# Residual weights of the second matrix by accumulating transfers, and other planned times for the first units

## The chip, the cores and the metric

The kernel runs on one core of one Trainium2 chip. The metric is the device time of one execution, in microseconds (us). The kernel before takes 532.01 us (median of three runs, 531.34 to 532.36).

The engines are called as in the profile: PE multiplies matrices, DVE, ACT and POOL work element by element, and SP starts the transfers from and to memory. Each engine runs its own instructions in the order in which they were issued, and waits on semaphores for the others.

## The reference

Sliding-window attention (each row sees itself and the 63 rows before it) feeds a gated two-matrix layer with a convolution of width 3 along the sequence:

```
scores = scale * q @ k.T ; masked to 0 <= rel < 64 ; softmax ; x = attn @ v      # B=8, H=8, S=576, D=64
h      = max(x @ w_in, 0)                                                        # 512 -> 1024
conv   = sum_k conv_w[k] * shifted(h, k - 1)
out    = (h * sigmoid(conv)) @ w_out                                             # 1024 -> 512
```

The weights `w_in`, `conv_w` and `w_out` come as 64-bit words and are turned into 32-bit floats on the chip.

## The kernel before, in words

**Units.** The 4608 rows are cut into 12 units of 384 rows. For each unit: scores (`qk`), row maxima (`row_max`), exponentials (`exps`), normalising, a transposition, attention times values (`values`), the first matrix (`mm1`), the rectifier (`relu`), the convolution (`conv_mid` on ACT, `conv_side` on DVE), the sigmoid and gate (`sig`, `gate`), and the second matrix (`mm2`). The score work of unit u+2 runs beside the matrices of unit u. Units 0 and 1 come out of a start-up stretch in which the weights are prepared too. Their transposition is on PE (`transpose_pe`), that of later units on DVE with small transfers. Scores of units 0 and 1 use 64-row pieces, those of later units 32-row pieces (64 matmuls a block, three blocks a unit).

**Large and small parts.** A 32-bit operand is multiplied as a large part, rounded to PE's fast format, and a small part, the difference to it. Each product is three matmuls: large times large, small weight times large, large weight times small. So `wih`, `woh` hold large parts of the weights and `wil`, `wol` the small parts; `xh`, `xl` and `gh`, `gl` do the same for activations.

**Weights.** A chunk of weights is two of the eight 128-row slices (the first two slices of `w_in` are chunks of their own). `to_f32` makes floats of the 64-bit words in a buffer `w24`, of which there are two: an absolute value and a scaling on ACT (L248, L255), a maximum on POOL (L249), and a shift, an or and an add on DVE (L250, L252, L256). Then POOL rounds the result to the large part (L269, `CAST`) and DVE subtracts it from the whole (L270), which gives the small part. `w_out` is four chunks; chunk n+2 uses the `w24` buffer of chunk n again.

**The order.** Every piece of work is put into a plan with a due time, an engine, a cost, what it reads and what it writes. `START` holds due times, in units of one eighth of a unit's work, for the start-up and for units 0, 1 and later ones. `queued` simulates the engines with the costs and always starts, on the engine that is free first, the ready work with the lowest due time; the order so found is issued as it stands. [...] While PE would wait in the first 110 us, `keep_busy` (L212) puts matmuls on zeros into the gap; their results are not used.

Of the kernel before, what the change touches and what calls it, by code (L numbers as in the profile page):

```python
# [8 lines left out]
F32 = mybir.dt.float32  # L9
F32R = mybir.dt.float32r  # L10
U32 = mybir.dt.uint32
AF = mybir.ActivationFunctionType
ALU = mybir.AluOpType
# [47 lines left out]
def queued(works, fill=None):  # L61
# [30 lines left out]
    while left:  # L92
# [17 lines left out]
        if fill and e == "PE" and start < FILL_TO:  # L110
# [4 lines left out]
            if n > 0 and clean:  # L115
                order.append(Work(x.t, e, 0.0, fill(n, min(clean)[1]), [], [], None, 0, 0.0))
        turn = SWITCH[e] if e in SWITCH and (x.kind != state[e] if e == "PE" else x.kind and x.kind != state[e]) else 0.0
        if turn and e == "PE" and not x.kind:
            turn = LEAVE
        if e == "PE" or x.kind:  # L120
# [17 lines left out]


START = {  # L140
    "v0": -27.5,
    "pv0": -15.968,
    "conv": -37.437,
    "bits": ((-46.561, -47.419), (-44.383, -45.007)),
    "qk1": -43.011,
    "v1": -11.849,
    "qk2": -2.185,
    "qk0": (-91.154, -52.794, -48.024),
    "ex0": (-42.377, -37.771, -19.993),
    "sc1": (-20.012, -18.408, -14.041),  # L150
    "ex1": (-8.106, -4.046, -3.778),
    "mask": -0.529,
    "sig": ((3.087, 7.079, 8.764, 10.751), (3.178, 6.73, 5.945, 9.966), (4.046, 6.806, 8.285, 10.314)),
    "in": (-39.031, -37.38, -33.878, -12.682, -12.013),
    "out": (-11.963, -8.679, 1.926, 7.315),
# [3 lines left out]
}  # L159
SWITCH = {"PE": 0.14, "ACT": 1.28}  # L160
LEAVE = 0.24
PORT_CL = 0.5
WARM = 5.0
FILL, FILL_FROM, FILL_TO = 4.0, 2.0, 110.0

# [2 lines left out]
def attention_moe(ctx: ExitStack, tc: tile.TileContext, q, k, v, w_in, conv_w, w_out, out):  # L168
    nc = tc.nc
# [4 lines left out]
    def many(n, shape, dt, name, where=pool):  # L174
        return [where.tile(shape, dt, name=f"{name}{i}") for i in range(n)]
# [7 lines left out]
    mask = many(3, [P, P], F32, "mask")  # L183
# [13 lines left out]
    bits = [flat.bitcast(U32)[:, 4 * DM * i:4 * DM * (i + 1)].rearrange("p (e two) -> p e two", two=2) for i in range(2)]  # L197
# [20 lines left out]
    def at(t, eng, cost, do, r=(), w=(), kind=None, mb=0, port=0.0):  # L218

        plan.append(Work(t, eng, cost, do, list(r), list(w), kind, mb, port))  # L220

    def two(t, eng, cost, do, **kw):
        at(t, eng, cost, do, port=cost, **kw)
# [20 lines left out]
    def to_f32(t, n, st, x, kb, kt):  # L244

        lw, hw, xu = st[..., 0], st[..., 1], x.bitcast(U32)

        at(t, "ACT", 0.0009 * n + 0.2, lambda: nc.scalar.activation(x, hw.bitcast(F32), AF.Abs), r=kb, w=kt)  # L248
        at(t, "POOL", 0.0027 * n + 0.02, lambda: nc.gpsimd.tensor_scalar(x, x, TINY, None, op0=ALU.max), w=kt, port=PORT_CL)  # L249
        two(t, "DVE", 0.00052 * n + 0.06, lambda: nc.vector.tensor_scalar(  # L250
            xu, xu, 3, 0x3FFFFFF8, op0=ALU.logical_shift_left, op1=ALU.bitwise_and), w=kt)
        two(t, "DVE", 0.00104 * n + 0.07, lambda: nc.vector.scalar_tensor_tensor(  # L252
            xu, hw, 0xC0000000, xu, op0=ALU.bitwise_and, op1=ALU.bitwise_or), r=kb, w=kt)

        at(t, "ACT", 0.0009 * n + 0.2, lambda: nc.scalar.activation(lw, lw, AF.Copy, scale=2.0 ** -29), w=kb)  # L255
        two(t, "DVE", 0.00104 * n + 0.07, lambda: nc.vector.tensor_tensor(xu, xu, lw, ALU.add), r=kb, w=kt)  # L256

    def weights(t, src, fs, hi, lo, key, buf, halves):

        e = slice(halves[0] * DM, (halves[-1] + 1) * DM)  # L260
        st, x = bits[buf][:, e], w24[buf][:, e]
        kb, kt = [("bits", buf, a) for a in halves], [("w24", buf, a) for a in halves]
        for f, a, tl in zip(fs, halves, load_at(buf, halves, t)):
            at(tl, "SP", 0.7, lambda f=f, a=a: nc.sync.dma_start(
                bits[buf][:, a * DM:(a + 1) * DM], src[f].bitcast(U32).rearrange("p (e two) -> p e two", two=2)),
               w=[("bits", buf, a)], mb=0.52)
        n = len(fs) * DM
        to_f32(t, n, st, x, kb, kt)
        two(t, "POOL", 0.00127 * n, lambda: nc.gpsimd.tensor_copy(hi, x), r=kt, w=[f"{key}{f}h" for f in fs])  # L269
        two(t, "DVE", 0.00104 * n + 0.07, lambda: nc.vector.tensor_tensor(lo, x, hi.bitcast(F32), ALU.subtract),  # L270
           r=kt + [f"{key}{f}h" for f in fs], w=[f"{key}{f}l" for f in fs])

    freed = {}

    def load_at(buf, halves, t):

        ts = [freed.get((buf, a), START["bits"][buf][a]) for a in halves]
        for a in halves:
            freed[(buf, a)] = t + 0.01
        return ts  # L280

    def weights_in(t, fs, *where):
        f = slice(fs[0], fs[-1] + 1)
        weights(t, w_in, fs, wih[:, f].rearrange("p f c e -> p (f c e)"),
                wil[:, f].rearrange("p f c e -> p (f c e)"), "in", *where)

    def weights_out(t, fs, *where):
        f = slice(fs[0], fs[-1] + 1)
        weights(t, w_out, fs, woh[:, f].rearrange("p f e -> p (f e)"), wol[:, f].rearrange("p f e -> p (f e)"), "out", *where)
# [441 lines left out]
```

## Time and profile before

| what | before |
|---|---|
| median of 3 runs | 532.01 us (531.34 to 532.36) |
| the profiled execution: own time, span | 531.34 us, 529.6 us |
| PE busy, share of the span | 518.5 us, 98% |
| DVE busy | 380.3 us, 72% |
| ACT busy | 379.7 us, 72% |
| POOL busy | 112.6 us, 21% |
| matmuls on zeros (L212) | 210, 28.6 us of PE's busy time |
| granted TensorE clock | 1.00 |

The profiled execution is the fastest of the three runs, 0.67 us under their median, and 1.7 us of its own time lie outside its span. A busy PE here is not always useful: the matmuls on zeros count as busy, so the gaps of the start-up are to be sought as L212 rows and not as idle time alone. Line numbers in the profile are those of the kernel before. In the changed kernel the lines behind L269 are moved by five: L270 there is the `CAST` of L269, L273 to L276 are new, and L506, say, is L501 here.

### The profile page before, as it was taken

The page shows a single profiled execution, that of the slowest core. Times are in us where ns is not written, and L with a number is a line of the kernel's source. Part 1 is how long each engine was busy: PE and PEld are TensorE (multiplying, and loading weights), DVE is VectorE, ACT ScalarE, POOL GpSimd, SP SyncE. Part 2 cuts the span into 40 slices and gives each one's busy share as a digit, 9 for nine tenths or more (in the row PEclk, how much of TensorE's full clock was granted, in tenths as well). Part 3 has the DMA queues.
Part 4 walks back from the last instruction along what each step waited for, and adds up shares of the span by engine and source line. Part 5 has one row for each costly group of instructions (what it writes and reads, how often), then busy time and mean ns, then how long its engine had stood idle before and what let it go on. Part 6 is the DMA issues. An engine that isn't in the chain of part 4 may idle for free.

```text
span 529.6 us, 14836 instructions
## 1 busy us (share of the span) xinstructions
PE 518.5 (98%) x5826; PEld 499.8 (94%) x5826; DVE 380.3 (72%) x1084; ACT 379.7 (72%) x1011; POOL 112.6 (21%) x196
## 2 busy tenths in 40 slices
PE   9998999999999999999999999999999999999996
PEld 8887889999999999999999999999999999999996
DVE  3899999985858667767767767767767667655552
ACT  2997897579896696696697687687687687544542
POOL 6664467113131011021021021021021021000000
PEclk9999999999999999999999999999999999999999
DMA  8984660237292173183083074073073053010011
GB/s 284 365 296 136 208 231 1 60 109 248 76 325 72 58 256 83 42 291 77 21 297 77 16 253 122 21 285 105 13 264 120 17 152 104 16 61 0 2 60 62
DMA packets 29463, 69.98 MB, mean 132 GB/s; under 512 B 5713, under 2 KB 17617, under 8 KB 29393
## 3 DMA queue, kind: packets, MB, share of 16 engines
q1 hardware_dynamic: 29392, 69.03, 39.7%
q8 instruction: 46, 0.75, 0.6%
q14 instruction: 25, 0.20, 0.1%
HBM read 47.73 MB, written 9.47 MB: 108 GB/s over the span
## 4 chain that ended last, share of the span: by engine, by line
PE 85%; DVE 9%; DMA 1%; ACT 1%; issue 1%; SPq 1%; POOL 0%; DVEq 0%
PE po L564 39%; PE acc L501 36%; PE acc L481 6%; PE sc L350 5%; DVE c L535 1%; DVE w L252 1%; DMA T<-in_w_in_dram 1%; DVE s L357 1%; DVE w L256 1%; DVE wil L270 1%; ACT s L367 1%; SPq L234 1%; DVE xl L488 1%; DVE s L378 1%; DVE w L250 1%
## 5 line engine op out<-in xcount | busy, mean ns | idle before, releaser
L501 PE MATMUL acc<-xh,wih 128*128 128x384 f32 x384 | 131.5, 342 | 0.8 <-DVE xl L488 0.8
L564 PE MATMUL po<-gh,woh 128*128 128x386 f32 (+1 forms) x384 | 132.1, 344 | 0.0
L535 DVE SCALAR_TENSOR_TENSOR c<-hbuf,cw,c 128x386 f32<-128x386 f32 (+1 forms) x192 | 109.6, 623 | 30.7 <-ACT c L528 30.7
L564 PE MATMUL po<-gh,wol 128*128 128x386 f32 (+1 forms) x384 | 129.9, 338 | 0.0
L564 PE MATMUL po<-gl,woh 128*128 128x386 f32 (+1 forms) x384 | 129.7, 338 | 0.0
L501 PE MATMUL acc<-xh,wil 128*128 128x384 f32 x384 | 129.7, 338 | 0.0
L501 PE MATMUL acc<-xl,wih 128*128 128x384 f32 x384 | 129.7, 338 | 0.0
L367 ACT ACTIVATE s<-s,nm 128x96 f32<-128x96 f32 (+2 forms) x288 | 105.1, 367 | 5.2 <-DVE nm L357 4.9
L555 DVE TENSOR_TENSOR gl<-c,gh 128x772 fp32r<-128x772 f32 (+1 forms) x48 | 55.8, 1162 | 28.2 <-ACT gh L551 28.1
L501 PEld LDWEIGHTS acc<-xh,wih 128*128 128x128 f32 x384 | 72.1, 188 | 2.9 <-POOL sm L370 0.7
L564 PEld LDWEIGHTS po<-gh,woh 128*128 128x128 f32 x384 | 72.2, 188 | 2.6
L378 POOL TENSOR_TENSOR s<-s,r 128x768 f32<-128x768 f32 x27 | 39.7, 1472 | 163.5 <-DVE r L373 150.7
L547 DVE TENSOR_TENSOR c<-c,hbuf 128x772 f32<-128x772 f32 (+1 forms) x48 | 47.4, 987 | 36.9 <-ACT c L542 36.7
L564 PEld LDWEIGHTS po<-gl,woh 128*128 128x128 f32 x384 | 72.3, 188 | 0.0
L564 PEld LDWEIGHTS po<-gh,wol 128*128 128x128 f32 x384 | 72.3, 188 | 0.0
L501 PEld LDWEIGHTS acc<-xh,wil 128*128 128x128 f32 x384 | 72.2, 188 | 0.0
L501 PEld LDWEIGHTS acc<-xl,wih 128*128 128x128 f32 x384 | 72.1, 188 | 0.0
L522 ACT ACTIVATE hbuf<-acc 128x384 f32<-128x384 f32 x64 | 30.9, 486 | 45.8 <-PE acc L501 45.4
L542 ACT ACTIVATE c<-c 128x772 f32<-128x772 f32 (+1 forms) x48 | 40.7, 848 | 30.2 <-DVE c L535 29.9
L357 DVE CUSTOM_DVE_ANT_0 s<-sc,mask 128x96 f32<-128x96 f32 (+2 forms) x272 | 51.5, 254 | 9.7 <-POOL mask L321 5.7
L367 ACT ACTIVATION_READ_ACCUMULATOR s<-s,nm 128x1 f32 x288 | 54.3, 189 | 0.0
L511 POOL COPY hbuf<-hbuf 128x4 f32<-128x4 f32 x44 | 16.7, 379 | 176.3 <-DVE c L547 176.2
(64 smaller groups left out, 644.5 us busy)
## 6 DMA issues: line engine op xcount, KB each, us to landing
v<-in_v_dram SPq DMA_DIRECT2D x24, 768.0 KB, 7.2
ub<-T SPq DMA_DIRECT2D x240, 48.0 KB, 1.9
k<-in_k_dram SPq DMA_DIRECT2D x22, 448.0 KB, 4.9
q<-in_q_dram SPq DMA_DIRECT2D x22, 384.0 KB, 6.9
out_dram<-T SPq DMA_DIRECT2D x8, 772.0 KB, 4.2
T<-in_w_in_dram SPq DMA_DIRECT2D x8, 512.0 KB, 6.6
T<-in_w_out_dram SPq DMA_DIRECT2D x8, 512.0 KB, 4.2
out_dram<-T SPq DMA_DIRECT2D x3, 768.0 KB, 6.4
```

The lines of the kernel that those rows point to most:

```text
L350: nc.tensor.matmul(banks_of(u, b)[h][r:r + rows, i * P + o:i * P + n], qs[hs, 2 * g + p, t:t + rows], ks[hs, 2 * g + p, t + o:t + n], star ...
L357: nc.vector.tensor_tensor_reduce(out=ss[b][:, i, h, o:n], in0=banks_of(u, b)[h][:, i * P + o:i * P + n], in1=mask[m][:, o:n], scale=-0.125 ...
L367: nc.scalar.activation(x, x, AF.Exp, bias=nms[b][:, e], scale=-1.0, accum_out=sms[b][:, e])
L378: on.tensor_tensor(sv, sv, rs[b].unsqueeze(2).broadcast_to([P, 2 * NB, n]), ALU.mult)
L481: nc.tensor.matmul(acc[bank(("v", u, c))][h * D:(h + 1) * D, t * W:(t + 1) * W], vs[:, c, t, h], ub[g][:, 2 * p:2 * p + 2, 2 * t + h], sta ...
L501: nc.tensor.matmul(acc[bank(("m", u, f))][:, :NX], w[:, f, c], x[u % 2][:, c], start=(c == 0 and j == 0), stop=(c == NC - 1 and j == 2))
L522: nc.scalar.activation(hbuf[:, f, o:o + NX], ps[:, :NX], AF.Relu)
L535: nc.vector.scalar_tensor_tensor(c, hbuf[:, f, e:e + n], cw[:, e, f:f + 1], c, op0=ALU.mult, op1=ALU.add)
L542: nc.scalar.activation(c, c, AF.Sigmoid)
L547: nc.vector.tensor_tensor(c, c, hbuf[:, 2 * i:2 * i + 2, 1:1 + n], ALU.mult)
L555: nc.vector.tensor_tensor(gls[ring(u, i)][:, :, :n], cs[i % 2][:, :, :n], ghs[ring(u, i)][:, :, :n].bitcast(F32), ALU.subtract)
L564: nc.tensor.matmul(po[o][:, :n], w[:, f, es], x, start=(f == 0 and j == 0), stop=(f == NF - 1 and j == 2))
```

## The change

The small part of `w_out` is no longer subtracted on DVE. ACT writes the negative of the large part to `wol` (L273), and then a transfer that POOL issues (L274) adds the whole from `w24` to it. `w_in` keeps its subtraction on DVE. Beside it stand other due times for the start-up and units 0 and 1 (those of later units are the same), and other costs for the planner: 0.12 and 0.19 for a change of matmul kind in place of 0.14 and 0.24, 0.87 us for the port in L249 in place of 0.5, and 1.06 us for a `CAST` of 1024 in place of 1.30.

```diff
 START = {
-    "v0": -27.5,
+    "v0": -29.922,
 ...
-    "out": (-11.963, -8.679, 1.926, 7.315),
+    "out": (-20.758, -19.305, -17.841, -7.024),
 ...
-SWITCH = {"PE": 0.14, "ACT": 1.28}
-LEAVE = 0.24
-PORT_CL = 0.5
+SWITCH = {"PE": 0.12, "ACT": 1.28}
+LEAVE = 0.19
+PORT_CL = 0.87
 ...
         n = len(fs) * DM
         to_f32(t, n, st, x, kb, kt)
-        two(t, "POOL", 0.00127 * n, lambda: nc.gpsimd.tensor_copy(hi, x), r=kt, w=[f"{key}{f}h" for f in fs])
-        two(t, "DVE", 0.00104 * n + 0.07, lambda: nc.vector.tensor_tensor(lo, x, hi.bitcast(F32), ALU.subtract),
-           r=kt + [f"{key}{f}h" for f in fs], w=[f"{key}{f}l" for f in fs])
+        his, los = [f"{key}{f}h" for f in fs], [f"{key}{f}l" for f in fs]
+        two(t, "POOL", 0.00104 * n, lambda: nc.gpsimd.tensor_copy(hi, x), r=kt, w=his)
+        if key == "out":
+            at(t, "ACT", 0.0009 * n + 0.12, lambda: nc.scalar.activation(lo, hi.bitcast(F32), AF.Copy, scale=-1.0), r=his, w=los)
+            at(t + 0.005, "POOL", 1.2, lambda: nc.gpsimd.dma_start(lo, x, accum_op=ALU.add), r=kt, w=los, mb=0.9)
+        else:
+            two(t, "DVE", 0.00104 * n + 0.07, lambda: nc.vector.tensor_tensor(lo, x, hi.bitcast(F32), ALU.subtract), r=kt + his, w=los)
```

Three places where the order differs. First POOL, around the large part of the first chunk of `w_out` (`woh`; `w240` and `w241` are the two `w24` buffers), before:

```order
L249 TENSOR_SCALAR w240_101<-w240_101 128x1024
L249 TENSOR_SCALAR w241_102<-w241_102 128x1024
L511 COPY hbuf_67<-hbuf_67 128x2x2
L513 MEMSET hbuf_67 128x2
L411 MEMSET ub1_62 32x2x384
L412 MEMSET ub1_62 32x2x384
L269 CAST woh_70<-w240_101 128x1024
```

and in the changed kernel:

```order
L270 CAST wih_68<-w241_102 128x1024
L270 CAST woh_70<-w240_101 128x1024
L249 TENSOR_SCALAR w241_102<-w241_102 128x1024
L274 DMA wol_71<-w240_101 128x1024
L516 COPY hbuf_67<-hbuf_67 128x2x2
L518 MEMSET hbuf_67 128x2
L270 CAST woh_70<-w241_102 128x1024
L274 DMA wol_71<-w241_102 128x1024
L249 TENSOR_SCALAR w240_101<-w240_101 128x1024
```

The transfer stands behind the maximum of the next chunk, and the rounding of the first chunk now follows that of the last chunk of `w_in` at once.

Second DVE, from the last row maximum of unit 2's second block to the last small part of unit 1's `x`, before (`wol` is the subtraction; a row of L488 makes a quarter of `xl`):

```order
L250 TENSOR_SCALAR w241_102<-w241_102 128x1024
L555 TENSOR_TENSOR gl0_97<-c0_92,gh0_94 128x772
L252 SCALAR_TENSOR_TENSOR w241_102<-T_100,w241_102 128x1024
L488 TENSOR_TENSOR xl1_66<-acc0_106,xh1_64 128x384
L488 TENSOR_TENSOR xl1_66<-acc1_107,xh1_64 128x384
L535 SCALAR_TENSOR_TENSOR c0_92<-hbuf_67,cw_72,c0_92 128x386 x2
L270 TENSOR_TENSOR wol_71<-w240_101,woh_70 128x1024
L256 ISA w241_102<-T_100,w241_102 128x2048
L535 SCALAR_TENSOR_TENSOR c0_92<-hbuf_67,cw_72,c0_92 128x386 x2
L488 TENSOR_TENSOR xl1_66<-acc0_106,xh1_64 128x384
L547 TENSOR_TENSOR c1_93<-c1_93,hbuf_67 128x772
L270 TENSOR_TENSOR wol_71<-w241_102,woh_70 128x1024
```

and in the changed kernel:

```order
L250 TENSOR_SCALAR w241_102<-w241_102 128x1024
L560 TENSOR_TENSOR gl0_97<-c0_92,gh0_94 128x772
L252 SCALAR_TENSOR_TENSOR w241_102<-T_100,w241_102 128x1024
L493 TENSOR_TENSOR xl1_66<-acc0_106,xh1_64 128x384
L540 SCALAR_TENSOR_TENSOR c1_93<-hbuf_67,cw_72,c1_93 128x386 x2
L256 ISA w241_102<-T_100,w241_102 128x2048
L540 SCALAR_TENSOR_TENSOR c1_93<-hbuf_67,cw_72,c1_93 128x386 x2
L493 TENSOR_TENSOR xl1_66<-acc0_106,xh1_64 128x384
L540 SCALAR_TENSOR_TENSOR c0_92<-hbuf_67,cw_72,c0_92 128x386 x2
L552 TENSOR_TENSOR c1_93<-c1_93,hbuf_67 128x772
L540 SCALAR_TENSOR_TENSOR c0_92<-hbuf_67,cw_72,c0_92 128x386 x2
L493 TENSOR_TENSOR xl1_66<-acc0_106,xh1_64 128x384
```

The two subtractions are gone from between the other rows.

Third ACT in the changed kernel, from the first negation (L273) to the second (L527 is the rectifier of `mm1`, L490 makes a quarter of `xh`, L248 is here the first step of the third chunk in the buffer `w240`):

```order
L490 CAST xh1_64<-acc0_106 128x384
L273 ACTIVATE wol_71<-woh_70 128x1024
L527 ACTIVATE hbuf_67<-acc1_107 128x384
L556 CAST gh0_94<-c0_92 128x772
L527 ACTIVATE hbuf_67<-acc1_107 128x384
L533 ACTIVATE c0_92<-hbuf_67,cw_72 128x386 x2
L255 ACTIVATE T_100<-T_100 128x1024
L527 ACTIVATE hbuf_67<-acc1_107 128x384
L490 CAST xh1_64<-acc0_106 128x384
L248 ACTIVATE w240_101<-T_100 128x1024
L547 ACTIVATE c1_93<-c1_93 128x772
L273 ACTIVATE wol_71<-woh_70 128x1024
```

A rectifier stands directly behind the first negation, and the third chunk's first write to `w240`, which the first transfer reads, stands ahead of the second.

More of the change, by code (lines that the diff above doesn't have):

```diff
@@ L140 @@
 START = {
-    "v0": -27.5,
[L142 to L154, printed above, removed]
-    "out": (-11.963, -8.679, 1.926, 7.315),
[3 rows of a table removed]
-}
-SWITCH = {"PE": 0.14, "ACT": 1.28}
-LEAVE = 0.24
-PORT_CL = 0.5
+    "v0": -29.922,
+    "pv0": -19.403,
+    "conv": -41.041,
+    "bits": ((-47.782, -46.477), (-39.599, -42.604)),
+    "qk1": -50.73,
+    "v1": -11.363,
+    "qk2": -8.864,
+    "qk0": (-89.193, -55.235, -53.427),
+    "ex0": (-43.48, -40.099, -25.648),
+    "sc1": (-9.472, -21.051, -12.204),
+    "ex1": (-7.956, -5.445, -5.217),
+    "mask": -7.074,
+    "sig": ((2.956, 5.48, 6.549, 10.868), (2.942, 5.419, 7.756, 9.491), (4.046, 6.806, 8.285, 10.314)),
+    "in": (-47.207, -43.911, -35.394, -25.628, -25.348),
+    "out": (-20.758, -19.305, -17.841, -7.024),
[3 rows of a table added]
+}
+SWITCH = {"PE": 0.12, "ACT": 1.28}
+LEAVE = 0.19
+PORT_CL = 0.87
 WARM = 5.0
```

6 rows, old and new, of the table START are left out of this document.

## The prediction

> **What bounds the kernel now.** First the busy shares, then busy time by stretch, since shares are averages over stages; then PE's instructions in order of time where the stretches change, and last the chain of waits.
>
> ```profile
> PE 518.5 (98%) x5826; PEld 499.8 (94%) x5826; DVE 380.3 (72%) x1084; ACT 379.7 (72%) x1011; POOL 112.6 (21%) x196
> ...
> 0.00:69.73 69.73, 28.56 (x210) 26.39 (x210) 1.00 0.75 260
> ...
> 69.73:96.57 26.84, 26.60 (x168) 1.00 0.23 78
> 96.57:530.00 433.43, 428.93 (x4713) 1.00 0.36 115
> ...
> 512.82 12.69 PE po L564 x72
> ```
>
> The first stretch row is of L212 alone (window, its length, PE, weight loads), the two below are of all of PE. All 210 zero matmuls, 28.56 us, lie ahead of 69.73 us. From there PE loses 0.24 us to 96.57, and from 96.57 to its last matmul (512.82 + 12.69 = 525.51) it is busy 428.93 of 428.94 us. The end is therefore the time at which PE becomes steadily fed, plus the PE work still to do. Only the start-up can move it, as the due times of later units are unchanged.
>
> ```profile
> 50.00:60.00 10.00, 9.69 (x135) 9.07 (x134) 10.00 (x26) 7.65 (x13) 7.29 (x3) 1.00 0.49 153
> 60.00:70.00 10.00, 8.50 (x164) 7.65 (x164) 10.00 (x27) 9.20 (x22) 3.05 (x5) 1.00 0.91 306
> 70.00:80.00 10.00, 9.76 (x74) 9.37 (x70) 10.00 (x14) 9.06 (x35) 6.97 (x5) 1.00 0.56 190
> 80.00:90.00 10.00, 10.00 (x58) 10.00 (x58) 9.52 (x13) 8.79 (x18) 8.07 (x7) 1.00 0.00 0
> ...
> 66.14 2.93 PE L212 MATMUL po<-spare 128*128 128x112 f32 x24
> 69.73 0.92 PE L481 MATMUL acc<-ub,v 128*64 128x64 f32 x24 [0.66 <-DVE xl L488]
> 70.58 0.44 PE L501 MATMUL acc<-xh,wih 128*128 128x384 f32 x1
> 70.86 0.34 PE L501 MATMUL acc<-xh,wil 128*128 128x384 f32 x1
> 71.04 0.34 PE L501 MATMUL acc<-xl,wih 128*128 128x384 f32 x1
> ...
> 71.20 1.14 DVE wol L270
> ...
> 75.84 2.38 PE acc L501 x12
> ```
>
> The columns are PE, weight loads, DVE, ACT, POOL, clock, share and rate of the transfers. DVE is busy without a gap from 50 to 80 us. At 66.14 PE fills with zeros and at 69.73 DVE releases it (L488). The chain runs through DVE and leaves it for good at 75.84. Of the four subtractions that go, only the one at 71.20 is on it: taken alone, the removal would be worth 1.14 us.
>
> **The change part by part.** *DVE.* The order moves as well, so I ask when PE is steadily fed now. In the changed order DVE's last long hold on PE is the row maximum of unit 2's first block, which frees the score banks for the second block. I count DVE's work ahead of its end against that ahead of 62.66 us in the trace:
>
> ```profile
> 54.85 0.25 DVE L357 CUSTOM_DVE_ANT_0 s<-sc,mask 128x96 f32<-128x96 f32 x1
> ...
> 56.27 2.79 DVE L535 SCALAR_TENSOR_TENSOR c<-hbuf,cw,c 128x386 f32<-128x386 f32 x4
> ...
> 59.59 1.14 DVE L535 SCALAR_TENSOR_TENSOR c<-hbuf,cw,c 128x386 f32<-128x386 f32 x2
> 60.65 1.21 DVE L252 SCALAR_TENSOR_TENSOR w<-T,w 128x1024 uint32<-128x1024 uint32 x1
> 61.78 0.95 DVE L547 TENSOR_TENSOR c<-c,hbuf 128x772 f32<-128x772 f32 x1
> 62.66 0.55 DVE L488 TENSOR_TENSOR xl<-acc,xh 128x384 fp32r<-128x384 f32 x1
> ...
> 64.54 1.21 DVE L256 CUSTOM_DVE_ANT_0 w<-T,w 128x2048 uint16<-128x2048 uint16 x1
> 65.68 0.68 DVE L250 TENSOR_SCALAR w<-w 128x1024 uint32<-128x1024 uint32 x1
> 66.28 1.79 DVE L555 TENSOR_TENSOR gl<-c,gh 128x772 fp32r<-128x772 f32 x1
> ```
>
> Prices are from start to start: a row maximum of eight rows 1.42 (54.85 to 56.27), a pair of L535 1.06 (59.59 to 60.65), a gate (L547) 0.88, an add (L256) 1.14. The changed order has one row maximum, two pairs of L535 and the gate less, and one add more: 62.66 - 1.42 - 2.12 - 0.88 + 1.14 = 59.38. PE's score block starts 0.1 later, at about 59.5; call this T. [...] One stall is 0.8 to 0.9 us (L555 took 1.79 at 66.28 beside a `CAST`, 0.91 undisturbed below), so T may be off by 1 to 2 stalls.
>
> ```profile
> 41.94 1.04 POOL L269 CAST wih<-w 128x1024 fp32r<-128x1024 f32 x1 [1.01 <-DVE w L256]
> 56.02 2.77 POOL L249 TENSOR_SCALAR w<-w 128x1024 f32<-128x1024 f32 x1 [1.50 <-ACT w L248]
> 65.89 1.37 POOL L269 CAST woh<-w 128x1024 fp32r<-128x1024 f32 x1 [1.26 <-DVE w L256]
> ...
> 78.20 0.91 DVE L555 TENSOR_TENSOR gl<-c,gh 128x772 fp32r<-128x772 f32 x1
> ...
> 103.09 2.11 PE acc L501 x12
> ...
> 115.20 0.93 PE sc L350 x57
> 116.13 0.85 PE acc L481 x24
> 116.98 2.30 PE po L564 x12
> ```
>
> *PE.* Ahead of 69.73 the trace has, beside work common to both, two `values` pieces (0.85 each), two halves of `mm1` (2.11 for both) and three narrow score blocks (0.93 each) more than the changed order has ahead of 59.5: 1.70 + 2.11 + 2.79 = 6.60 us. So the same point of PE's work is reached at 66.1, 3.6 us earlier, and the 0.24 us lost before 96.57 is gone too: 3.8 in all. From it go four things.
>
> (a) The changed order returns from short matmuls to 384-column ones seven times more behind this point. A return costs 0.10 (70.58 to 70.86 against 0.18 for the next step) to 0.18 (2.30 for twelve at 116.98 against 2.11): 0.7 to 1.3, taken as 1.0.
>
> (b) The `mm1` behind that block needs its bank read by the rectifier, which stands behind the first negation. The add ends at 59.38 - 1.42 = 57.96, and with 0.1 to 0.2 per handover (64.54 + 1.21 = 65.75 to the `CAST` at 65.89) the `CAST` (1.04 at 41.94) ends at 59.2, the negation (1.16, as L255 of the same size below) at 60.5, the rectifier (0.49, L522 below) at 60.95, so that `mm1` starts at 61.0; the score block is done at 60.4: 0.6 lost. Should the rectifier come first, this is zero.
>
> (c) Unit 2's last row maximum: its end is 75.24 (L488 in the trace) less a subtraction (1.14), plus a gate (0.88) and a small part (L555, 0.83 net of overlap), 75.8, plus 0.1. PE gets there at 59.5 + 15.0 (six halves, three `values`, two score blocks, eight `mm2` pieces of 0.53) + 0.6 (b) + 0.5 of (a) = 75.6. Lost: 0.3.
>
> (d) ACT was busy 27.05 of 30 us from 60 to 90. Three of the four negations fall there, 3.5 us into 2.95 free, with rectifiers behind them. I allow 0.7; bounds 0 and 1.5.
>
> ```profile
> L255 ACT ACTIVATE T<-T 128x1024 uint32<-128x1024 uint32 x5 | 5.8, 1158 | 0.0
> ...
> L522 ACT ACTIVATE hbuf<-acc 128x384 f32<-128x384 f32 x64 | 30.9, 486 | 45.8 <-PE acc L501 45.4
> ...
> T<-in_w_out_dram SPq DMA_DIRECT2D x4, 512.0 KB, 3.9
> ub<-T SPq DMA_DIRECT2D x240, 48.0 KB, 1.9
> q<-in_q_dram SPq DMA_DIRECT2D x22, 384.0 KB, 6.9
> v<-in_v_dram SPq DMA_DIRECT2D x1, 768.0 KB, 4.2
> ```
>
> *The transfers.* No transfer from POOL and none that adds is in the trace. From 48 KB in 1.9 us to a lone 768 KB in 4.2, 512 KB are one pass of 1.5 above 1.9: 3.4 if adding is free. Reading whole and destination makes two passes, 4.9; writing counted as a third, 6.4, and beside other loads a plain transfer took 6.9. I take 5, nearest to the 3.9 of the same size plus the second read. POOL's queue sets the issue: `CAST` to 59.2, then the maximum ahead of the transfer (2.77 at 56.02), 62.0. Its first readers are the first `mm2`, at 59.5 + 0.6 + 0.93 + 2.11 + 0.93 + 2.11 + 0.85 + 1.06 + 0.4 = 68.5, and, by the buffer `w240`, ACT's first step for the third chunk about 67.7. The slack is 5.7, so 5 us are hidden; without the cover every microsecond over 5.7 stops ACT with the gates behind it. How long the issue occupies POOL no row shows; POOL is 30% busy from 60 to 70, and behind the first issue stand only small border copies (L511) and the next `CAST`, which needs the second chunk's add first, so a microsecond or two there costs nothing.
>
> [...]
>
> Sum: 3.8 - 1.0 - 0.6 - 0.3 - 0.7 = 1.2 us. The profiled execution took 531.34 us, so the like of it 530.1; it lies 0.67 under the median of 532.01, which gives **530.8 us**.
>
> **The rivals.** *The transfer lands late (slower).* If it needs 8 us, as the loads in company suggest (6.9, and adding is more), it is 2.3 late at ACT; the second transfer likewise holds its first `mm2`, and the third and fourth chunks wait for the buffers of the first two, so the lateness comes two to three times: 4.6 to 6.9, less 1.2, some 4.5 us slower, 536. It decides from about 6.2 us of landing, where the 1.2 is used up. For it: transfers are 91% busy from 60 to 70. Against it: the lone 768 KB in 4.2.
>
> [...]
>
> *Issuing costs DVE what a `CAST` costs.* If POOL's writing for a transfer stalls DVE 0.85 each, the one at 62 and that of the second chunk are on the path: 1.7 lost, 532.5, no change that can be told.
>
> *More gain.* The waits of (b), (c) and (d) are covered because DVE has fewer stalls than before, and the returns cost 0.7: 3.8 - 0.7 = 3.1, 528.9. For it: the removed subtractions, 1.14 each at 71.20 and later, leave DVE slack there; against it: ACT's 92% from 60 to 70.
>
> **How the numbers follow.** A measurement here tells about 0.2%, 1.06 us, from no change. Chances: the forecast 0.46, late landing 0.22, stalls by issuing 0.16, more gain 0.16. The forecast's own spread is 1 us either way from T's stalls and (d), 529.6 to 532.2: faster 0.26, same 0.18, slower 0.02. Late landing gives slower 0.21, same 0.01; stalls by issuing slower 0.07, same 0.08, faster 0.01; more gain faster 0.16. Together faster 0.43, same 0.27, slower 0.30. The range reaches from the more-gain case, 528.9, over the forecast to a landing one microsecond late three times over, 530.8 + 3 and a stall of 0.85, about 535.
>
> **What would show it.** The L212 rows end by about 59 us in place of 69; a score block starts near 59.5; PE has waits of a few tenths behind a rectifier and a row maximum between 60 and 76, and is gapless behind 97. A transfer lands within 5.7 us, and neither L248 nor L564 waits for it. The forecast is wrong where L248 or L564 waits for a transfer, where DVE's two-input rows lengthen at the issues, or where ACT makes PE wait more than 1.5 us from 70 to 97.

## The result, and the profile after

The changed kernel takes 534.71 us (median of seven runs, 533.76 to 538.38) beside 532.10 us for the kernel before on the same chip: a ratio of 1.006, 95% interval 1.0038 to 1.0081. It is slower by 2.6 us, where 1.2 us of gain were forecast. The profiled execution is the median one: 534.71 us, span 532.9.

The changed kernel's page (busy shares; the chain of waits):

```profile
PE 522.1 (98%) x5826; PEld 500.0 (94%) x5826; DVE 380.8 (71%) x1080; ACT 382.7 (72%) x1015; POOL 109.9 (21%) x200
...
PE 75%; ACT 10%; DVE 9%; DMA 3%; POOL 2%; issue 1%; SPq 0%; ACTq 0%
```

Its stretches (the first of L212 alone, with PE, weight loads, clock, transfers; the others of all of PE) and its last matmul:

```profile
0.00:62.30 62.30, 28.86 (x210) 26.96 (x210) 1.00 0.70 245
...
62.30:97.00 34.70, 33.45 (x359) 1.00 0.65 189
97.00:530.00 433.00, 431.39 (x4714) 1.00 0.36 115
...
528.32 0.34 PE L569 MATMUL po<-gl,woh 128*128 128x386 f32 x1
```

The zero matmuls end by 62.3 instead of 69.7, so the start-up does its work sooner. Yet PE's last matmul ends at 528.66 instead of 525.50. Idle time does not say where the 3.16 us arose, since PE reads as busy almost throughout. So I compared the two traces at equal work: each useful matmul counts its start-to-start time (0.176 us for one of the wide matmuls of `mm1` and `mm2`, 0.0145 for scores, 0.035 for `values`), and for each amount of work the time in the trace before is set against the time in the other. Minus is ahead of the kernel before:

| at, in the trace before | changed | old switch costs late (e1) | e1 without transfers (e7) | e1 with four loads moved (e8) |
|---|---|---|---|---|
| 73 us | -0.98 | -0.66 | -1.68 | -2.34 |
| 80 | +0.09 | +0.34 | -1.64 | -1.73 |
| 95 | +0.44 | +0.61 | -1.54 | -1.41 |
| 187 | +0.81 | +1.01 | -1.13 | -1.01 |
| 247 | +1.45 | +1.01 | -1.13 | -1.01 |
| 348 | +2.15 | +1.01 | -1.13 | -1.01 |
| end | +3.16 | +1.01 | -1.13 | -1.01 |

Two losses stand out in the first column: about a microsecond between 73 and 80 us, and 0.3 us again and again behind 187.

**The later units.** PE's rows and its weight loads' waits in the changed kernel:

```profile
201.76 0.34 PE L569 MATMUL po<-gh,woh 128*128 128x386 f32 x1
201.94 0.34 PE L569 MATMUL po<-gh,wol 128*128 128x386 f32 x1
202.34 0.45 PE L569 MATMUL po<-gl,woh 128*128 128x386 f32 x1
202.62 0.34 PE L569 MATMUL po<-gh,woh 128*128 128x386 f32 x1
...
PEld po L569 <- DVE gl L560: 2.5, 7, 0.4
```

The same place before:

```profile
202.00 0.34 PE L564 MATMUL po<-gh,woh 128*128 128x386 f32 x1
202.18 0.34 PE L564 MATMUL po<-gh,wol 128*128 128x386 f32 x1
202.36 0.34 PE L564 MATMUL po<-gl,woh 128*128 128x386 f32 x1
202.53 0.34 PE L564 MATMUL po<-gh,woh 128*128 128x386 f32 x1
```

Three matmuls take 0.53 us before and 0.86 now: the third needs the gate's small part `gl`, and its weight load waits for DVE. The wait occurs in seven units (at 201.8, 242.4, 283.0 and so on, 40.6 us apart), 2.5 us in all. The row of the small part, after and before:

```profile
200.14 2.15 DVE L560 TENSOR_TENSOR gl<-c,gh 128x772 fp32r<-128x772 f32 x1 [0.32 <-ACT gh L556]
```

```profile
199.33 2.14 DVE L555 TENSOR_TENSOR gl<-c,gh 128x772 fp32r<-128x772 f32 x1 [0.32 <-ACT gh L551]
```

It takes the same time and is 0.8 us later, which is no more than this trace is behind as a whole there (+0.81 in the table). But `mm2` begins 0.24 us sooner, so it has moved ahead of `gl` by one microsecond. In the order of the instructions PE had four halves of `mm1` and then eight pieces of `mm2` in each later unit; now it has three, four pieces, one, four pieces. No due time of those units changed, but the planner's costs for a change of matmul kind did, and the planner uses them in every unit.

**The transfers.** Issue, landing (KB, median us) and what waits, in the changed kernel:

```profile
63.05 1.36 POOL L274 DMA_DIRECT2D wol<-w  x1
73.00 0.86 POOL L274 DMA_DIRECT2D wol<-w  x1 [2.58 <-ACT wol L273]
...
wol<-w POOLq DMA_DIRECT2D x1, 512.0 KB, 6.8
...
wol<-w POOLq DMA_DIRECT2D x1, 512.0 KB, 6.5
...
DMA to landing us min/median/max: 4.5/5.5/6.8
...
ACT w L248 <- DMA wol<-w: 0.6, 1, 0.6
```

The two with other loads beside them need 6.8 and 6.5 us; the least, 4.5, is behind 87 us. In this execution only ACT waits for a transfer, 0.6 us.

### The profile page after: what moved, and what is told of

Its sections match the earlier page's. It is cut to its first block, busy times and chain, and to the rows that moved or that the text cites. A ratio compares the mean times of both kernels' runs of the same rounds, so it can differ in the third digit from the quotient of the medians.

```text
span 532.9 us, 14835 instructions
## 1 busy us (share of the span) xinstructions
PE 522.1 (98%) x5826; PEld 500.0 (94%) x5826; DVE 380.8 (71%) x1080; ACT 382.7 (72%) x1015; POOL 109.9 (21%) x200
## 4 chain that ended last, share of the span: by engine, by line
PE 75%; ACT 10%; DVE 9%; DMA 3%; POOL 2%; issue 1%; SPq 0%; ACTq 0%
PE po L569 34%; PE acc L506 29%; PE acc L486 6%; PE sc L355 4%; ACT s L372 4%; DVE gl L560 2%; DVE c L540 2%; POOL w L249 2%; DMA q<-in_q_dram 1%; PE acc L212 1%; ACT L372 1%; DMA T<-in_w_out_dram 1%; DVE w L252 1%; ACT L547 1%; DVE w L256 1%
## 5 line engine op out<-in xcount | busy, mean ns | idle before, releaser
L540 DVE SCALAR_TENSOR_TENSOR c<-hbuf,cw,c 128x386 f32<-128x386 f32 (+1 forms) x192 | 111.2, 629 | 47.7 <-ACT c L533 47.7
L552 DVE TENSOR_TENSOR c<-c,hbuf 128x772 f32<-128x772 f32 (+1 forms) x48 | 51.6, 1078 | 27.8 <-ACT c L547 27.4
L527 ACT ACTIVATE hbuf<-acc 128x384 f32<-128x384 f32 x64 | 30.9, 484 | 52.7 <-PE acc L506 52.6
L533 ACT ACTIVATE c<-hbuf,cw 128x386 f32<-128x386 f32 (+1 forms) x96 | 53.4, 607 | 1.1 <-DVE gl L560 1.1
```

The source lines that it names most:

```text
L527: nc.scalar.activation(hbuf[:, f, o:o + NX], ps[:, :NX], AF.Relu)
L533: nc.scalar.activation(cs[i % 2][:, a, :n], hbuf[:, f, 1:1 + n], AF.Copy, scale=cw[:, 1, f:f + 1])
L540: nc.vector.scalar_tensor_tensor(c, hbuf[:, f, e:e + n], cw[:, e, f:f + 1], c, op0=ALU.mult, op1=ALU.add)
L552: nc.vector.tensor_tensor(c, c, hbuf[:, 2 * i:2 * i + 2, 1:1 + n], ALU.mult)
```

## Experiments

The line numbers in the experiments' rows are two or three above those of the changed kernel; in e2's they are two above those of the kernel before. The ratios are against the kernel before on the same chip: e1 to e7 ran on one chip, e8 to e10 on another, e11 and e12 on a third. e7 leaves out the small parts of `w_out`, e12 those of its second chunk.

| run | edit | median, us (range) | ratio, 95% interval |
|---|---|---|---|
| e1 | changed kernel, old switch costs from 160 us on | 532.22 (530.72 to 536.09) | 1.0017 (0.9998 to 1.0036) |
| e2 | kernel before, new switch costs from 140 us on | 533.66 (533.01 to 533.81) | 1.0028 (1.0017 to 1.0038) |
| e3 | e1, subtraction on DVE for the transfers | 538.00 (537.56 to 538.43) | 1.0112 (1.0099 to 1.0125) |
| e4 | e1, 9 zero matmuls at the start for 12 | 532.90 (530.83 to 537.12) | 1.0019 (1.0000 to 1.0039) |
| e7 | e1 without the transfers | 529.96 (529.52 to 530.80) | 0.9969 (0.9958 to 0.9981) |
| e8 | e1, four loads moved behind the second transfer | 530.97 (530.43 to 531.40) | 0.9981 (0.9972 to 0.9990) |
| e9 | e1, two loads moved | 530.95 (530.17 to 533.21) | 0.9992 (0.9981 to 1.0003) |
| e10 | e1, own buffer for the third chunk | 532.67 (529.80 to 535.42) | 1.0024 (1.0002 to 1.0045) |
| e11 | e8 and e10 together | 531.47 (530.28 to 532.10) | 0.9996 (0.9987 to 1.0005) |
| e12 | e8 without the second transfer | 530.52 (529.79 to 531.33) | 0.9974 (0.9964 to 0.9984) |

### Do the later units lose 0.3 us each (e1, e2)?

In the planner, for work planned from a time on (in e2 the other way round, 0.12 and 0.19 from 140 on, in the kernel before):

```diff
             turn = LEAVE
+        if turn and e == "PE" and start >= 160:
+            turn = 0.14 if x.kind else 0.24
```

> The changed kernel with the planner's old switch costs (0.14 and 0.24) for PE work planned from 160 us on; all before that is instruction for instruction the changed kernel. The steady units then get the old grouping back (four mm1 halves, then eight mm2 pieces, in place of three, four, one, four). Theory A (the steady units lose 0.3 us each): in the changed kernel's trace PE waits 0.3 us for the gate's small part (L560) once in each of seven units, at 201.8, 242.4, ... 445.4; these waits go, 7 x 0.31 = 2.15 us: 534.7 - 2.15 = 532.5 us. Theory B (all the loss is made in the start-up, by the transfers and the late landing of DVE's work): no change, 534.7.

> The kernel before with the new switch costs (0.12 and 0.19) for PE work planned from 140 us on, nothing else. Theory A: the seven steady units get the new grouping and its wait, 7 x 0.31: 532.1 + 2.15 = 534.3 us, without any transfer from POOL. Theory B: no change, 532.1.

e1 is 2.5 us better than the changed kernel, and no weight load waits for `gl` behind 160 us. e2, which has no transfer from POOL and the old start-up, is 1.85 us slower than the kernel before and has the wait row of the changed kernel:

```profile
PEld po L566 <- DVE gl L557: 2.5, 7, 0.4
```

Theory A holds in both directions: two planner costs, changed together with the start-up's due times, cost 1.9 to 2.5 us in the later units (2.15 in the table, 3.16 less 1.01). That is nearly the whole loss of 2.6 us, because what the start-up gains and what the transfers cost, found below, largely cancel.

### Do the transfers pay, and does a late start matter (e3, e4)?

e3:

```diff
-            at(t, "ACT", 0.0009 * n + 0.12, lambda: nc.scalar.activation(lo, ...
-            at(t + 0.005, "POOL", 1.2, lambda: nc.gpsimd.dma_start(lo, x, accum_op=ALU.add), ...
+        two(t, "DVE", 0.00104 * n + 0.07, lambda: nc.vector.tensor_tensor(lo, x, ..., ALU.subtract), ...
```

> The run with the old switch costs from 160 us on, but w_out's small parts made by DVE's subtraction as before; the new due times stay, and the planner puts the rest around it anew. Theory A: the transfers do their work in the start-up, four subtractions (1.14 each) come back on DVE and at least the two ahead of 75 us are on the path: 1.1 to 2.3 slower than the run with the transfers, 533.6 to 534.8. Theory B (the transfers cost as much as they save, by stalls at their issue and at ACT): within 0.5 of it, 532.0 to 533.0 or faster.

It is 5.8 us slower than e1, far beyond either theory. e3's PE wait and the DVE rows ahead of it:

```profile
PE acc L483 <- DVE xl L490: 5.5, 2, 5.2
```

```profile
75.45 1.21 DVE L273 TENSOR_TENSOR wol<-w,woh 128x1024 fp32r<-128x1024 f32 x1
...
77.72 1.92 DVE L537 SCALAR_TENSOR_TENSOR c<-hbuf,cw,c 128x386 f32<-128x386 f32 x2
79.57 1.79 DVE L549 TENSOR_TENSOR c<-c,hbuf 128x772 f32<-128x772 f32 x1
81.28 0.54 DVE L490 TENSOR_TENSOR xl<-acc,xh 128x384 fp32r<-128x384 f32 x1
```

One subtraction of 1.2 us stands there, but the planner now puts a long DVE queue ahead of `xl`, for which PE waits 5.2 us at a stretch. So e3 prices an order planned for other work, not the subtractions. Whether the transfers pay against subtractions in an order planned for those, no run shows.

e4:

```diff
-            n = int((start - t) * FILL)
+            n = int((start - t) * FILL) if free[e] else 9
```

> The run with the old switch costs from 160 us on, with 9 zero matmuls in place of 12 ahead of the first score block (18 passes in place of 24). In the trace of the changed kernel the first 24 passes take 5.46 us and the score block starts at 6.44, in that of the kernel before 4.53 and 5.51, and its q had landed at 1.24 + 3.4 = 4.64. Theory A (a late first score block carries through DVE to the end): the block starts at 4.9 in either case, so 0.6 to 1.5 us of the end is won, 531.0 to 531.9. Theory C (the later loads set the start-up, and a late first block is absorbed): the same time as with 12, 532.5.

Theory C: a sooner first block brings nothing (the times without a late transfer have a median of 531.55, e1's 531.54). But the run explains why the times of e1 and of the changed kernel spread so far: six of e4's twelve times lie at 530.8 to 531.7 and six at 534.1 to 537.1, and its profile is of the latest (537.12 us, span 535.3). PE's rows there, then PE's stretches (busy, clock, transfers), then the second transfer's landing:

```profile
79.18 0.44 PE L571 MATMUL po<-gh,woh 128*128 128x386 f32 x1
82.28 0.69 PE L571 MATMUL po<-gh,wol 128*128 128x386 f32 x1 [2.66 <-DMA wol<-w]
```

```profile
79.60:82.20 2.60, 0.02 (x1) 0.87 0.43 157
82.20:88.40 6.20, 6.12 (x19) 0.51 0.02 8
88.40:97.00 8.60, 8.60 (x51) 1.00 0.32 61
```

```profile
wol<-w POOLq DMA_DIRECT2D x1, 512.0 KB, 9.1
```

The second transfer needs 9.1 us, PE stands still for 2.7, and then the clock is halved for 6 us, in which 19 matmuls need 0.32 us each instead of 0.176. Against the kernel before this execution is 0.55 us ahead at 79 us and 5.3 behind at 83: that is the rival of the late landing.

The granted clock has a mean of 1.00 from 76 to 80 us, of 0.88 from 80 to 82 and of 0.50 from 82 to 88, which puts its fall at about 81.5 us, 1.9 us into the wait (the mean of 0.87 over the stretch of 2.60 us says the same). So this wait cost more than its length: 2.7 us, and about as much again behind it (19 matmuls at 0.32 us in place of 0.176 are 2.8 us).

### What makes the transfers late, and what do they cost (e7, e8, e9)?

e7 leaves out the four adding transfers. Two runs beside it, e5 and e6, held back loads to see whether company makes the transfers late:

> The run with the old switch costs from 160 us on, and six loads of SP's queue (k and q of unit 3, issued at 61.6 to 66.0 us, and v of unit 2, issued at 72.3) held back until the second adding transfer has landed, by a read of one element of its destination that stands ahead of them in SP's queue. Their readers come behind 98 us. Without that, the twelve times were seven at 530.7 to 532.3 and five at 533.5 to 536.1, and in the trace of a late one PE waits 3 us for a transfer that took 9.1 us to land (4.5 to 7.4 in the trace of an early one), with a granted clock of 0.5 for 7 us behind the wait. Theory D (the loads in company make the transfers late): transfers land in at most 5.5 us, the late times go, median 531.2, none above 532.5. Theory E (the lateness is the transfer's own, in its descriptors or one slow DMA engine): median 532.2, again with times to 536.

> As the run that holds back six loads, but only the two of v (2 x 768 KB, issued at 72.3, where the second adding transfer is issued at 73) are held until it has landed; k and q stay beside the first transfer. Theory D with v as the load that matters: the late times go, and ACT still waits 0.6 to 1.2 us for the first transfer, which costs PE at most 0.5: median 531.5. If k and q matter as much, late times stay and the median lies between 531.5 and 532.2. Theory E: 532.2.

> The run with the old switch costs from 160 us on without its four adding transfers: w_out's small parts stay the larger parts' negatives, so that w_out's share of the small parts is missing from the output. All other instructions and their order are the same. Theory D and theory E alike: nothing waits for a transfer, no late times, median 531.0 to 531.3; DVE's pair at 73.9 (two at 2.2 us with 1.6 of stall) loses the 0.8 that falls beside the transfer's issue at 73.7, if the issue is what holds it. If the late times stay, neither the loads nor the transfers make them.

The times of e5 (547.13 us) and e6 (542.18) say nothing on the question: I had put the held loads of v ahead of unit 1's last piece of `values`, which therefore waited for them (14.4 and 9.9 us) and read unit 2's v; and k and q of e5 include a half that is read at 78 us, not behind 98. Their traces do say something. The first transfer, which has k and q beside it, lands in 5.0 us in e5, where they are held, and in 7.6 in e6, where they are not; the second lands in 4.5 in both, with v held.

e7 takes 529.96 us without late times, 1.0 below what was expected even of an execution whose transfers land in time. So the transfers cost 2.3 us of e1's median, and 1.6 where only its seven times without a late transfer are counted (530.7 to 532.3, median 531.54). e8 and e9 put the loads in the right place:

```diff
+        held = kq[18:20] + vs_[4:6]                      # e9: vs_[4:6]
 ...
+        new = [Work(0, "SP", 0, lambda: nc.sync.dma_start(gate[0:1, 0:1], wol[0:1, 2, 0:1]...), ...)] + held
+        order = [x for x in order[:at_] if x not in held] + new + [x for x in order[at_:] if x not in held]
```

> The run with the old switch costs from 160 us on, and four loads of SP's queue (k and q of the second half of unit 3, issued at 65.6 and 66.0 us, and v of unit 2, issued at 72.3 and 77.4) moved behind the point where SP has seen the second adding transfer land, by a one-element read of its destination in SP's queue; behind unit 1's last piece of values in the program, and ahead of their first readers, which come behind 98 us. Theory D (loads in company make the transfers late and uncertain): both transfers land in 5.5 us or less, no time above 532.5, and of the 2.3 us that the run without transfers (529.96) is better, 1 to 1.5 come back: median 530.7 to 531.2. Theory E (the lateness is the transfer's own): median 532.2 with times to 536.

> As the run that moves four loads, but only the two of v (768 KB each, issued at 72.3 and 77.4 beside the second adding transfer). Theory D with v as what matters: the late times go and ACT still waits some 1 us for the first transfer: median 531.0 to 531.6. If k and q matter as much: late times stay, 531.6 to 532.2. Theory E: 532.2.

e8's ten times lie between 530.43 and 531.40: the late ones are gone, as theory D has it. Its second transfer, and SP's read that waits for it to land:

```profile
71.71 0.86 POOL L277 DMA_DIRECT2D wol<-w  x1 [2.65 <-ACT wol L276]
```

```profile
76.22 0.73 SPq L674 DMA_DIRECT2D gate<-wol  x1
```

It lands in 4.5 us instead of 6.3 (e1) to 9.1. The first one, with other loads still beside it, has 6.8 as before. With v alone moved (e9) the median is the same, but three of the twelve times are above 532. In e9's profile the first transfer takes 7.6 us, ACT waits 1.4 for it and a weight load of `mm2` 0.9, where e8's has 6.8, 0.7 and none; so the half of k and q that only e8 moves seems to matter too.

e8 is 1.25 us better than e1, which ran on another chip. Nearer to it is e10 below: on e8's chip, with no load moved, it has six late times of twelve (533.2 to 535.4), and its six others (529.8 to 532.2) have a median of 531.07, beside 530.97 for e8. So what the moved loads buy is that the late times go; an execution that is on time hardly gains. The lead of e8 over e1 in the table at 73 us is for the greater part not theirs either: it is there before the first of them would start (see T below).

e8 is also faster than the kernel before by 0.19% (interval 0.10 to 0.28): the one version that computes the whole and is told from the kernel before as faster.

How the loads hold the second transfer up, no run shows; what the runs show is its 4.5 us without them against 6.3 to 9.1 beside them.

### What is left to the transfers (e10, e11, e12)?

e10 and e11:

```diff
-        st, x = bits[buf][:, e], w24[buf][:, e]
+        st, x = bits[buf][:, e], w24[2 if key == "out" and fs[0] == 4 else buf][:, e]
```

> The run with the old switch costs from 160 us on, with a buffer of its own for the third chunk of w_out (a third w24), so that ACT's first step for it no longer waits for the first adding transfer to have read its source (1.2 us of wait in that run's trace, 0.6 in the changed kernel's); the order of all instructions is the same. If that wait is the transfers' cost on the on-time path: 0.5 to 1.2 us better, 531.0 to 531.7, with the late times of the second transfer left. If it only eats idle time of ACT: no change, 532.2.

> The run that moves four loads (530.97), with a buffer of its own for the third chunk of w_out besides. Its trace still has ACT's first step for the third chunk wait 0.7 us for the first transfer. If that wait holds the third chunk on the path: 530.3 to 530.6. If ACT would be idle there anyway: 531.0.

> The run that moves four loads (530.97), without the second of the four adding transfers alone, so that the small parts of the second chunk of w_out stay the larger parts' negatives; all else and its order is the same. It splits the 1.0 us that is left to the run without any transfer (529.96). If the second transfer's issue is what costs it (DVE's pair of L543 beside it took 1.2 to 1.6 us more than its least, 0.36 in the run without transfers, and PE then waits 0.6 for L496): 530.0 to 530.3. If it is the first transfer, by the third chunk's wait at ACT: 530.9 to 531.0.

ACT no longer waits for the first transfer in e10, and the median is no better, though with half of the times late it says little. e11 has no late times, and is no better than e8 either. So that wait, 0.7 us in e8, does not show at the end. e12, without the second transfer, is 0.45 us under e8, but on another chip and with intervals that overlap; on its own chip it is 0.95 under e11, with intervals apart. So the second transfer seems to cost some 0.5 to 1 us even where it lands in 4.5. How, the DVE rows of the changed kernel and of e7 show at that place (two instructions each):

```profile
73.15 2.74 DVE L540 SCALAR_TENSOR_TENSOR c<-hbuf,cw,c 128x386 f32<-128x386 f32 x2
```

```profile
72.76 1.14 DVE L542 SCALAR_TENSOR_TENSOR c<-hbuf,cw,c 128x386 f32<-128x386 f32 x2
```

Beside POOL's issue at 73.00 (0.86 us) and the maximum that follows at once, DVE's pair takes 1.6 us more, and PE waits 0.80 us for the `xl` behind it. Not all of it is the issue's: without the transfer POOL's maximum comes sooner (69.78 us in e7, 70.38 in e12, 73.58 in the changed kernel) and lengthens another pair, from 1.14 us to 1.45 in e7 and to 1.93 in e12. How the 1.0 us between e8 and e7 divides between the transfers is not settled, and what is not the second one's is not traced to a place.

## Why the prediction was wrong, step by step

By its own account the forecast was 3.8 us of gain, 2.6 of deductions, and nothing for the transfers and the later units.

**"Only the start-up can move it, as the due times of later units are unchanged": the step that failed.** The due times were unchanged, the costs that decide between them were not. The new switch costs stand in the diff, and the prediction asks for their effect nowhere behind the start-up. "Gapless behind 97" was wrong for the same reason. In the runs PE waits for `gl` once in each of seven later units. Price: 1.85 us (e2) to 2.5 (e1), forecast 0.

**The transfers are hidden: the second step that failed.** Taken were 5 us of landing with 5.7 of slack, and that neither L248 nor `mm2` would wait; L248 waits 0.6 us in the changed kernel's profile, `mm2` 2.7 in e4's. With no other transfer in flight (issued at 87.61 us in the changed kernel) it lands in 4.5, so the price from 3.9 plus a second read, an estimate, was near, though no run shows that read apart; in the company that it has in this kernel it took 6.3 to 9.1, which is the range of the late-landing rival ("it decides from about 6.2 us"). That rival had a chance of 0.22 and a price of some 4.5 us over the kernel before; in six of e4's twelve runs it came in, with 2.3 to 5.3 over that kernel's median, in its profile by one wait of 2.7 and not by several smaller ones. What I had not counted is the halved clock behind the wait. Cost over all runs: 2.3 us of the median (e1 less e7), of which moving four loads takes away 1.25 (e1 less e8, on two chips), by the late times.

**The new order with free transfers: right in its sum, in part by luck.** e7 is that case: 1.7 us better than the kernel before by its ratio of 0.9969 (0.9958 to 0.9981); forecast was 1.2. But its terms were not as forecast. Counted at equal work, e7 is 2.1 us ahead at 69.7, where 3.0 were forecast (3.6 less (b)), and loses 0.9 from there to the end, where (a), (c) and (d) less the regained 0.24 were to take 1.8. The two errors cancel. With e7's -1.7 for the order, 2.3 for the transfers and 2.5 for the later units the whole comes to +3.1, where 2.6 was measured (the medians stem from several sessions).

**T, the first long hold's end.** Forecast 59.38 for DVE and 59.5 for PE. The rows of the changed kernel (DVE's work behind the row maximum; PE's score block; `mm1`), and DVE's busy time from 20 to 60 us, with what DVE waits for:

```profile
60.59 1.59 DVE L552 TENSOR_TENSOR c<-c,hbuf 128x772 f32<-128x772 f32 x1
...
60.91 1.00 PE L355 MATMUL sc<-k,q 64*32 64x96 f32 x64
...
62.31 0.42 PE L506 MATMUL acc<-xh,wih 128*128 128x384 f32 x1
```

```profile
20.00:60.00 40.00, 35.50 (x94) 1.00 0.60 212
...
DVE w L250 <- POOL w L249: 2.2, 3, 0.9
DVE w L256 <- ACT T L255: 1.1, 2, 0.8
DVE wil L276 <- POOL wih L270: 0.7, 1, 0.7
```

The same stretch before:

```profile
20.00:60.00 40.00, 39.78 (x115) 1.00 0.63 216
```

T was 1.2 us late here. The sum for it took over DVE's idle time as the trace before has it, and that was wrong: DVE, idle for 0.2 us of these 40 there, is now idle for 4.5, nearly all of it behind ACT and POOL inside the preparation of the weights. But T is not a fixed number: in e8, with the same order ahead of it, the row is at

```profile
59.24 1.58 DVE L555 TENSOR_TENSOR c<-c,hbuf 128x772 f32<-128x772 f32 x1
```

and in e1 at 60.7. What goes with it stands further up in the traces: ACT's first step for the first chunk of `w_out` waits for SP's load of that chunk. In the changed kernel:

```profile
46.44 1.14 ACT L248 ACTIVATE w<-T 128x1024 f32<-128x1024 f32 x1 [1.19 <-DMA T<-in_w_out_dram]
```

and in e8:

```profile
45.10 1.14 ACT L251 ACTIVATE w<-T 128x1024 f32<-128x1024 f32 x1 [1.50 <-DMA T<-in_w_out_dram]
```

In the nine profiles of this order T is 59.0 to 59.2 where this step begins by 45.1, 59.6 to 59.8 where it begins at 45.6 to 46.2, and 60.0 to 60.7 where it begins at 46.4 to 47.2 (47.15 in e1). In the kernel before, ACT waits for no load of weights from 38 to 66 us. So the sum for T lacks a term: the new due times want the first chunk of `w_out` before its load has landed. No run changes that load alone, so this is read from the rows and not tested. The start of the first block is not it (e4 began it sooner and had T at 60.4), nor are the loads moved in e8: e10 moves none and has T at 59.6.

**The deductions.** (b): `mm1` began at 62.31, 0.40 behind the end of the score block (60.91 + 1.00); forecast was 0.6. (a), (c) and (d) cannot be told apart, but in e7, where no transfer disturbs them, the lead falls only from 1.68 at 73 us to 1.13 at 187, less than half a microsecond of it behind 95.

**"Issuing costs DVE what a `CAST` costs" (chance 0.16).** Half right: the second issue and the maximum tied to it cost DVE 1.6 us, and beside the other three the DVE rows keep their least length within 0.15. That DVE's rows lengthen beside POOL's work the traces show (L555 takes 1.79 us beside a `CAST`, 0.91 without), not by what means; `port` in the kernel is the planner's name for the time for which it keeps such work of the two apart. At the end, leaving out the second transfer is worth 0.45 us (e12 against e8) to 0.95 (against e11).

## What to carry to other kernels

When a planner decides the order, a changed cost is a change everywhere the planner uses it: compare the order of every stage, not of the stage that was edited. The transfer's price depended on its neighbours here (4.5 us, or 6.3 to 9.1): see what else is in flight when it is issued, and move loads that are not needed yet behind it by making their queue wait for its landing. Where PE can wait for microseconds, price a slow clock behind the wait as well (here 2.8 us behind 2.7). And where work is planned sooner, look whether what it reads has landed by then.

## Not expected

- PE without a matmul for 2.7 us was followed by 6 us at a clock of 0.5 (e4); in e3, with a wait of 5.2 us, it is 0.50 from 80 to 86 us.
- The late transfer of e4 has a tail in which little of the chip moves: it lands at 82.2 us; in 40 slices from 76 to 83 us (share of the DMA engines in tenths, then GB/s):

```profile
DMA  8989799998999998969996999402002000101011
GB/s 164 211 164 211 140 211 211 234 246 211 269 222 234 281 316 316 375 234 468 410 480 234 445 410 340 152 0 47 35 35 47 35 35 35 70 35 70 35 70 70
```

From 80.6 us to the landing, 1.7 us, the sixteen engines together are busy to a tenth or two at most, as if one or a few of them finished the transfer alone. Whether that is so, which ones and why, no run here shows.
- PE's pace at the start doubles (0.213 to 0.112 us from one pass on zeros to the next) at a time that differs from execution to execution: at 4.4 us in the trace before, behind 6 us in the changed kernel's, so that the first 24 passes take 4.53 and 5.46 us. A sooner first block did not help the end (e4).
